# Half-unit, single-packet transfers for w_gate and w_up in a layer's forward and backward pass

## The chip, the cores and the metric

The kernel runs on one core of a Trainium2 chip. The metric is device time in microseconds (us) of the whole program, in runs without a disturbed clock; differences between kernels come from runs on the same chip in the same rounds. A profile is one execution under the hardware profiler. Its engines are PE (TensorE), DVE (VectorE), ACT (ScalarE), POOL (GpSimd) and SP (SyncE). Sixteen DMA engines move the data. Transfers reach them through three queues: q0, filled by GpSimd's software; q1, filled in hardware for SyncE; and q10, in hardware for ScalarE.

## The reference, cut to what matters

One token goes through a block with attention over the last 4096 positions of a cache and a gated feed-forward layer. Output and all gradients are wanted. Two gradients are of the whole cache, 4 heads x 65536 positions x 128, and are zero outside the last 4096 positions.

```python
# feed-forward part: D = 1024, F = 3584, all in bf16
g = einsum('bsd,df->bsf', x, w_gate)
u = einsum('bsd,df->bsf', x, w_up)
h = sigmoid(g) * u
y = einsum('bsf,fd->bsd', h, w_down)
...
_out, _vjp = jax.vjp(_f, A_x, A_k_cache, A_v_cache, A_wq, A_wo,
                     B_w_gate, B_w_up, B_w_down, c, w_mod)
return (_out, *_vjp(grad_out))
```

## The kernel before

Work is with single columns, so there is little arithmetic for each byte. Every weight is loaded once, used forward and backward, overwritten with its gradient in place, and stored. 120 stores of zeros (1024 KB each, rows of 8 KB) fill the cache gradients. They need no computed value and are spread over the program by hand-set lists: 61 go through GpSimd, some of them paced by a hand-set wait, and 59, in the feed-forward stage, through ScalarE without one.

The feed-forward stage has seven blocks of 512 columns. A *unit* is a block of one weight: 1024 KB. For w_gate and w_up it is 128 partitions x 8 rows of 1 KB. Five slots of 8 KB per partition are shared, so a load waits for the store of the gradient that was in its slot: w_gate of block n+1 for w_down's gradient of block n, w_up of n+2 for w_gate's, w_down of n+2 for w_up's.

```python
def load_wu(n):
    nc.gpsimd.dma_start(out=wu_t[n], in_=wu_view[:, :, n * FB:(n + 1) * FB])
def load_wg(n):
    nc.gpsimd.dma_start(out=wg_t[n], in_=wg_view[:, :, n * FB:(n + 1) * FB])
...
for n in range(NB):
    # ... PE: gate and up products; ACT: sigmoids; DVE: products; ACT: du_b, dg_b ...
    nc.sync.dma_start(out=wd_dram(out_8, n), in_=wd_t[n])     # w_down's gradient
    if n + 1 < NB:
        load_wg(n + 1)                                        # waits for that store
    for j in range(KD):
        ttr(wu[:, j, :], wu[:, j, :], du_b, dh2acc[...])      # DVE: row sums, backward
        last = outer_act(wu[:, j, :], h2[:, j:j + 1], du_b)   # ACT: the gradient, in place
        if j % 4 == 3:
            zero(Z_FFN[5 * n + 1 + j // 4], None, nc.scalar)  # zeros, issued by ACT
    nc.gpsimd.dma_start(out=dwu_view[:, :, n * FB:(n + 1) * FB], in_=wu)
    # ... the same for wg and dwg ...
    if n + 2 < NB:
        load_wu(n + 2)
        load_wd(n + 2)                                        # on SyncE
```

## Time and profile before

| | before |
|---|---|
| time, median of the first three runs | 653.28 us (651.76 to 654.0) |
| profiled span | 650.8 us |
| bytes moved | 262.63 MB |
| DMA engines busy, three queues together | 99.4% of the span |
| busiest compute engine (DVE) | 49% |

The page's first parts, its queues, its chain and the timeline of one block are shown in the prediction. Three more lines are from the list of transfers of the kernel before, with queue, count, size and the median time in us from issue to landing.

```profile
out_dram<-zeros ACTq DMA_DIRECT2D x59, 1024.0 KB, 20.9
arena<-in_B_w_up_dram POOLq DMA_DIRECT2D x7, 1024.0 KB, 14.5
arena<-in_B_w_gate_dram POOLq DMA_DIRECT2D x7, 1024.0 KB, 14.7
```

An estimate from the 425 GB/s that full slices of the GB/s row show: a unit of 1024 KB would take sixteen otherwise idle engines about 2.5 us. A w_gate load takes 14.7, as it shares them and queues behind others.

### The profile page before, as it was taken

The numbers are of one execution on the slowest core, as the hardware profiler recorded it, in microseconds if no ns is written. First come the engines' busy times: TensorE is split into PE (matmuls) and PEld (weight loads), VectorE is DVE, ScalarE is ACT, GpSimd is POOL, SyncE is SP. The second block draws the span as 40 slices with busy tenths as digits, with TensorE's granted clock in tenths as the row PEclk, the third lists the DMA queues.
The fourth block names the chain that finished last, engine by engine and source line by source line (L and its number), as shares of the span: only waits on it lengthen the run. The fifth ranks groups of instructions, "written<-read, shape, count | busy, mean of one in ns | idle before, by whom it ended". The sixth has DMA issues, their size and how long they took to land.

```text
span 650.8 us, 7106 instructions
## 1 busy us (share of the span) xinstructions
PE 149.7 (23%) x2784; PEld 127.4 (20%) x2784; DVE 319.7 (49%) x626; ACT 206.9 (32%) x306; POOL 83.0 (13%) x137
## 2 busy tenths in 40 slices
PE   3123227572201020010101101310670000424300
PEld 2123215572201020010101101300450000313200
DVE  3442005602737246081460814899700089996293
ACT  2000016611521613243133432789570000424800
POOL 2000000131010200102011010212111012112220
PEclk9999999865555555555555555575765555555555
DMA  8999999999999999999999999999999999999996
GB/s 335 430 428 422 426 426 413 404 418 397 421 425 415 416 417 393 414 388 408 417 356 419 361 409 415 392 382 412 388 415 422 415 425 426 425 407 388 410 411 251
DMA packets 43810, 262.63 MB, mean 404 GB/s; under 512 B 4096, under 2 KB 4096, under 8 KB 18432
## 3 DMA queue, kind: packets, MB, share of 16 engines
q0 software_dynamic: 23184, 131.08, 49.8%
q1 hardware_dynamic: 12048, 69.22, 26.0%
q10 hardware_dynamic: 8544, 61.88, 23.6%
q8 instruction: 22, 0.36, 0.2%
q14 instruction: 12, 0.10, 0.0%
HBM read 76.55 MB, written 185.60 MB: 403 GB/s over the span
## 4 chain that ended last, share of the span: by engine, by line
DMA 64%; DVE 14%; ACT 11%; PE 6%; issue 4%; POOL 0%; SPq 0%; POOLq 0%; ACTq 0%; DVEq 0%
DMA out_dram<-arena 28%; DMA arena<-in_B_w_gate_dram 18%; DMA arena<-in_w_mod_dram 7%; DVE arena L168 6%; DMA arena<-in_A_wq_dram 6%; ACT arena L172 5%; DMA arena<-in_A_k_cache_dram 5%; DVE junk L168 3%; PE tp_kv L342 2%; DVE arena L164 1%; ACT arena L345 1%; PE gu_ps L476 1%; ACT arena L230 1%; ACT du_b L508 1%; DMA out_dram<-dx_orow 1%
## 5 line engine op out<-in xcount | busy, mean ns | idle before, releaser
L168 DVE CUSTOM_DVE_ANT_0 arena<-arena 128x4096 bf16<-128x4096 bf16 (+1 forms) x24 | 80.1, 3350 | 51.4 <-DMA arena<-in_w_mod_dram 51.4
L476 PE MATMUL gu_ps<-h_bf,arena 128*128 128x1 bf16 x448 | 16.9, 172 | 192.1 <-DMA arena<-in_B_w_up_dram 103.5
L151 DVE TENSOR_TENSOR hh<-sg,gu_ps 128x4 f32<-128x4 f32 x7 | 1.1, 158 | 119.4 <-ACT om L481 119.4
L136 POOL DMA_DIRECT2D out_dram<-zeros x61 | 33.6, 554 | 185.0 <-PE q_ps L311 49.8
L476 PEld LDWEIGHTS <-arena 128*128 128x128 bf16 x448 | 16.2, 118 | 193.9 <-issue 166.7
L172 ACT ACTIVATE arena<-du_b,h 128x512 bf16<-128x512 bf16 x56 | 35.3, 710 | 36.0 <-DMA arena<-in_B_w_down_dram 32.3
L649 PEld LDWEIGHTS <-arena 8*128 8x128 bf16 x256 | 24.9, 127 | 106.1 <-issue 102.7
L172 ACT ACTIVATE arena<-dg_b,h 128x512 bf16<-128x512 bf16 x56 | 35.3, 708 | 26.4 <-issue 14.4
L345 ACT COPY arena<-tp_kv 128x1024 bf16<-128x1024 bf16 x13 | 13.1, 1010 | 89.7 <-PE tp_kv L342 89.7
L653 ACT CAST arena<-ps_kv 128x512 bf16<-128x512 f32 x32 | 16.1, 691 | 77.2 <-DMA out_dram<-arena 77.2
L168 DVE CUSTOM_DVE_ANT_0 junk<-arena,b1k 128x1024 bf16<-128x1024 bf16 x28 | 34.2, 1222 | 8.6 <-DMA arena<-in_B_w_down_dram 8.1
L168 DVE CUSTOM_DVE_ANT_0 arena<-arena,b1k 128x1024 bf16<-128x1024 bf16 x32 | 36.7, 1221 | 0.4 <-ACT b1k L230 0.4
L168 DVE CUSTOM_DVE_ANT_0 arena<-arena,du_b 128x512 bf16<-128x512 bf16 x56 | 34.8, 686 | 3.5 <-ACT du_b L508 3.5
L168 DVE CUSTOM_DVE_ANT_0 arena<-arena,dg_b 128x512 bf16<-128x512 bf16 x56 | 34.8, 685 | 0.0
L172 ACT ACTIVATE arena<-b1k,o_col 128x1024 bf16<-128x1024 bf16 x32 | 33.4, 1142 | 0.0
L649 PE MATMUL ps_kv<-DO_hd,arena 8*128 8x128 bf16 x128 | 15.3, 280 | 77.9 <-ACT arena L653 77.2
L342 PE MATMUL tp_kv<-ident_bf,arena 128*128 128x128 bf16 x256 | 22.1, 252 | 20.7 <-DMA arena<-in_A_k_cache_dram 13.0
L160 DVE COPY arena<-tp_kv 128x1024 bf16<-128x1024 bf16 x19 | 13.0, 690 | 28.1 <-PE tp_kv L342 28.1
L480 ACT ACTIVATE sg<-gu_ps 128x4 f32<-128x4 f32 x7 | 1.2, 174 | 76.3 <-PE gu_ps L476 76.3
L342 PEld LDWEIGHTS <-arena 128*128 128x128 bf16 x256 | 19.2, 115 | 23.6 <-DMA arena<-in_A_k_cache_dram 13.9
L429 POOL DMA_DIRECT2D arena<-in_B_w_up_dram x7 | 6.2, 890 | 134.4 <-DMA out_dram<-arena 134.4
L655 ACT ACTIVATE arena<-ps_kv 128x512 bf16<-128x512 f32 x32 | 16.1, 624 | 21.8 <-DMA out_dram<-arena 21.8
(185 smaller groups left out, 377.3 us busy)
## 6 DMA issues: line engine op xcount, KB each, us to landing
out_dram<-zeros POOLq DMA_DIRECT2D x61, 1024.0 KB, 20.4
out_dram<-zeros ACTq DMA_DIRECT2D x59, 1024.0 KB, 20.9
out_dram<-arena POOLq DMA_DIRECT2D x46, 1024.0 KB, 20.8
arena<-in_A_wq_dram SPq DMA_DIRECT2D x16, 1024.0 KB, 21.1
arena<-in_w_mod_dram SPq DMA_DIRECT2D x8, 1536.0 KB, 29.9
arena<-in_A_wo_dram SPq DMA_DIRECT2D x8, 1024.0 KB, 22.2
arena<-in_w_mod_dram SPq DMA_DIRECT2D x8, 1024.0 KB, 23.9
arena<-in_B_w_down_dram SPq DMA_DIRECT2D x7, 1024.0 KB, 11.9
```

The source lines that it names most:

```text
L136: ins = (q or nc.gpsimd).dma_start(out=zleft.pop(0), in_=zeros[:, :])
L160: return nc.vector.tensor_copy(out=out, in_=a)
L164: return nc.vector.tensor_scalar(out=out, in0=a, scalar1=s1, scalar2=None, op0=op0)
L168: return nc.vector.tensor_tensor_reduce(out=out, in0=w, in1=b, scale=1.0, scalar=0.0, op0=ALU.mult, op1=ALU.add, accum_out=acc)
L172: return nc.scalar.activation(out=out, in_=b, func=ACT.Copy, scale=col)
L230: last = nc.scalar.copy(out=o, in_=ps[:, :])
L342: nc.tensor.transpose(tp[:, t8 * P:(t8 + 1) * P], src[:, g, t_ * DH:(t_ + 1) * DH], ident_bf[:, :])
L345: last = nc.scalar.copy(out=o, in_=tp[:, :])
L476: nc.tensor.matmul(gu[:, half * 4 + jj:half * 4 + jj + 1], lhsT=w[:, j, jj::4], rhs=h2_bf[:, j:j + 1], start=(j == 0), stop=(j == KD - 1))
L649: nc.tensor.matmul(ps[:, t4 * DH:(t4 + 1) * DH], lhsT=rows[32 * g:32 * g + HG, t_ * P:(t_ + 1) * P], rhs=hd[32 * g:32 * g + HG, :], start= ...
L653: nc.scalar.copy(out=o, in_=ps[:, :])
L655: nc.scalar.activation(out=o, in_=ps[:, :], func=ACT.Copy, scale=float(scale))
```

## The change

The intent: with one packet for each engine's part of a half unit, the load should keep an engine for the whole of that packet instead of giving it up to zeros after each 4 KB; and a gradient's first half should leave while the second is being made. Half units keep a packet within 32 rows per engine.

```diff
     def load_wu(n):
-        nc.gpsimd.dma_start(out=wu_t[n], in_=wu_view[:, :, n * FB:(n + 1) * FB])
+        for k in range(0, KD, 4):
+            nc.gpsimd.dma_start(out=wu_t[n][:, k:k + 4, :], in_=wu_view[:, k:k + 4, n * FB:(n + 1) * FB],
+                                single_packet=True)
 ...  (load_wg likewise)
             if j % 4 == 3:
+                nc.gpsimd.dma_start(out=dwu_view[:, j - 3:j + 1, n * FB:(n + 1) * FB], in_=wu[:, j - 3:j + 1, :],
+                                    single_packet=True)
                 zero(Z_FFN[5 * n + 1 + j // 4], None, nc.scalar)
-        nc.gpsimd.dma_start(out=dwu_view[:, :, n * FB:(n + 1) * FB], in_=wu)
 ...  (dwg likewise)
```

More of the change, by code (lines that the diff above doesn't have):

```diff
@@ L428, in load_wu @@
     def load_wu(n):
-        nc.gpsimd.dma_start(out=wu_t[n], in_=wu_view[:, :, n * FB:(n + 1) * FB])
+        for k in range(0, KD, 4):
+            nc.gpsimd.dma_start(out=wu_t[n][:, k:k + 4, :], in_=wu_view[:, k:k + 4, n * FB:(n + 1) * FB],
+                                single_packet=True)
     def load_wg(n):
-        nc.gpsimd.dma_start(out=wg_t[n], in_=wg_view[:, :, n * FB:(n + 1) * FB])
+        for k in range(0, KD, 4):
+            nc.gpsimd.dma_start(out=wg_t[n][:, k:k + 4, :], in_=wg_view[:, k:k + 4, n * FB:(n + 1) * FB],
+                                single_packet=True)
     load_wd(0)
@@ L518 @@
             if j % 4 == 3:
+                nc.gpsimd.dma_start(out=dwu_view[:, j - 3:j + 1, n * FB:(n + 1) * FB], in_=wu[:, j - 3:j + 1, :],
+                                    single_packet=True)
                 zero(Z_FFN[5 * n + 1 + j // 4], None, nc.scalar)
-        nc.gpsimd.dma_start(out=dwu_view[:, :, n * FB:(n + 1) * FB], in_=wu)
         for j in range(KD):
@@ L524 @@
             if j % 4 == 3:
+                nc.gpsimd.dma_start(out=dwg_view[:, j - 3:j + 1, n * FB:(n + 1) * FB], in_=wg[:, j - 3:j + 1, :],
+                                    single_packet=True)
                 zero(Z_FFN[5 * n + 3 + j // 4], None, nc.scalar)
-        nc.gpsimd.dma_start(out=dwg_view[:, :, n * FB:(n + 1) * FB], in_=wg)
         if n + 2 < NB:
```

## The prediction

> **What bounds the kernel now.** I read the page's first two parts first, to see whether an engine or the transfers set the time; then the queues; then the chain of waits, which needs the first answer to be read properly; then the stage that the change touches, in the table by windows and the timeline.
>
> ```profile
> span 650.8 us, 7106 instructions
> PE 149.7 (23%) x2784; PEld 127.4 (20%) x2784; DVE 319.7 (49%) x626; ACT 206.9 (32%) x306; POOL 83.0 (13%) x137
> DMA  8999999999999999999999999999999999999996
> GB/s 335 430 428 422 426 426 413 404 418 397 421 425 415 416 417 393 414 388 408 417 356 419 361 409 415 392 382 412 388 415 422 415 425 426 425 407 388 410 411 251
> DMA packets 43810, 262.63 MB, mean 404 GB/s; under 512 B 4096, under 2 KB 4096, under 8 KB 18432
> q0 software_dynamic: 23184, 131.08, 49.8%
> q1 hardware_dynamic: 12048, 69.22, 26.0%
> q10 hardware_dynamic: 8544, 61.88, 23.6%
> ```
>
> No compute engine is over half busy, but the DMA row is at 9 nearly everywhere, and the three queues' packet times add to 99.4% of the sixteen engines' span. So the engines that move data are the bound, from the second slice to the last but one. At the good slices' 426 GB/s the 262.63 MB would take 616 us; the rest of the 651 us is slow moving rather than idleness. 120 of the transfers are stores of zeros, 1024 KB each, which depend on nothing but a place in a queue: they fill every gap.
>
> ```profile
> DMA out_dram<-arena 28%; DMA arena<-in_B_w_gate_dram 18%; DMA arena<-in_w_mod_dram 7%; DVE arena L168 6%; DMA arena<-in_A_wq_dram 6%; ACT arena L172 5%; DMA arena<-in_A_k_cache_dram 5%; DVE junk L168 3%; PE tp_kv L342 2%; DVE arena L164 1%; ACT arena L345 1%; PE gu_ps L476 1%; ACT arena L230 1%; ACT du_b L508 1%; DMA out_dram<-dx_orow 1%
> ```
>
> The chain names loads of w_gate (18%, 117 us), and reading it alone one would promise a large gain. But these loads are slow because zeros share the engines with them; the bytes remain.
>
> In the feed-forward stage, from the POOL and ACT timelines:
>
> ```profile
> 182.74 0.91 POOL L432 DMA_DIRECT2D arena<-in_B_w_gate_dram  x1 [21.52 <-DVE dhh L168]
> 183.64 0.90 POOL L520 DMA_DIRECT2D out_dram<-arena  x1
> 184.53 0.89 POOL L526 DMA_DIRECT2D out_dram<-arena  x1
> 213.32 0.89 POOL L429 DMA_DIRECT2D arena<-in_B_w_up_dram  x1 [27.90 <-DMA out_dram<-arena]
> 220.89 0.89 POOL L432 DMA_DIRECT2D arena<-in_B_w_gate_dram  x1 [6.68 <-DMA out_dram<-arena]
> 221.77 0.89 POOL L520 DMA_DIRECT2D out_dram<-arena  x1
> ...
> 184.27 8.91 ACTq L136 DMA_DIRECT2D out_dram<-zeros  x3
> 198.10 0.17 ACT L480 ACTIVATE sg<-gu_ps 128x4 f32<-128x4 f32 x1 [14.73 <-PE gu_ps L476]
> ```
>
> Two things are to be seen. POOL issues in program order: the w_up gradient is stored right after the next w_gate load (182.74 then 183.64; 220.89 then 221.77), and that load waits for the w_down gradient to land in the slot it needs. And ACT, which issues the zeros of this stage, is held for 8.91 us by three of them before it can do its next sigmoid.
>
> **What the Trainium skill says.** "DMA: Bandwidth & Descriptors", section "Queues, rings and completion order": each engine takes turns between queues by whole packets. The trace agrees: with w_gate or gradient packets of 4 KB on q0 against zeros of 8 KB on q10, in 187 to 205 us the packet records show 623 against 603, turn by turn, so q0 gets a third of the bytes. Section "SWDGE vs HWDGE vs iDMA" of the same page gives a packet as preferably up to 4096 B and at most 64 descriptors; in the trace the w_gate and w_up packets are 4096 B, four rows of 1 KB. Half a unit is 32 rows per engine, so it fits one packet of 32 KB. Section "Why small descriptors are slow" says that joining descriptors pays only up to 256 B; the trace has the numbers to check this, below. Its section "Rules for kernel authors" says that transfers issued from SP, ACT and GpSimd all run on the same 16 engines and interleave; the queue shares above agree.
>
> **The change part by part.**
> (a) Packet overhead. In the packet records the commonest durations are 84 ns for 2 KB, 159 for 4 KB, 309 for 8 KB and 460 for 12 KB: 150.5 ns per 4 KB and about 8.5 ns per packet. The 28 MB of w_gate, w_up and their gradients are 7168 packets of 4 KB; they become 896 of 32 KB. Saved: 6272 x 8.5 ns / 16 engines = 3.3 us. Against it, 28 more transfers each add one 9 ns completion packet per engine: 0.25 us. Net -3.1 us.
> (b) Share of an engine. A 32 KB packet takes about 8 x 150.5 + 8.5 = 1.21 us, against 0.31 us of a zero packet: q0 goes from a third to four fifths of the engine while it has work. A w_gate load now takes 14.7 us (median). It should take some 4.5 us from issue to its first packet (182.74 to 187 in the packet records), 2 x (1.21 + 0.31) = 3 us of moving, and some 2 us for the slowest engine: 9 to 10 us. Six loads on the chain save about 30 us of waiting there.
> (c) Where (b) goes. The zeros wait instead, and ACT holds them. Counting zeros issued against bytes moved on q10, the backlog never exceeds 6.6 MB before ACT stalls. Each unit block issues 4 to 11 zeros (59 in all), so in time its work is (6 + zeros) x 2.47 us at 425 GB/s: 35 to 42 us, against loop times of 38 to 41 us now. The chain can run ahead only until the backlog is full; then sigmoid and casts wait for zeros. I count zero net, except that the dip around 360 to 370 us, where the engines are about 89% busy, should fill: -1 us.
> (d) Reads that are no longer mixed. From 160 to 163 us almost only w_gate and w_up move, at 352 GB/s, 188 ns per 4 KB; mixed with zeros in 187 to 205 us they take 160 ns. With four fifths of the engine the loads are closer to alone. All 11 loads that come inside the loop at the slow rate would cost 11 x 16 x 28 ns = 4.9 us; I take half, +2.5 us.
> (e) Issue. A unit costs POOL 0.89 us, a zero 0.53; a half should be about 0.7, so +14 us of POOL in a stage of 245 us in which it is busy 20 us. Off the path: 0.
> (f) "Leaves as soon as made": POOL comes to the first stores only after the w_gate load, by which time most of both gradients is made. What ACT finishes late (2.92 us of waiting at 225.58) gains a little, behind a busy queue: 0.
> (g) The slot of w_down is free sooner, since its load waits for the w_up gradient to land; it moves out of the way of the w_down store. Chain shorter, bytes the same: 0, as in (c); perhaps -1 us for less waiting at the stage's end.
> Sum: -3.1 - 1 + 2.5 - 1 = -2.6 us: 650 to 651 us.
>
> **The rivals.** First, the chain decides: (b) and (g) come through and the loop falls to 30 us or less; the time would be 610 to 630. For it speaks the 18% of the chain; against it the 99.4% of packet time, since nothing in the change removes bytes. Second, better mixing cures the slow spells. The table by windows has 321 GB/s for 246 to 249 us at full occupancy, and packet times in this stage exceed their usual values by 10 us; if large packets removed most of that, 641 to 643. Against it: similar spells fall at 455 and 570 us, outside this stage, around the start of a load on q1 among stores. Third, the other way: long packets hold back q1, whose w_o rows go in 2 KB packets and whose w_down loads and stores are on the path, or ACT is held so long that first halves come late and the engines run empty: +5 to +12 us, 658 to 665.
>
> **Range and chances.** The bound is shown by three views, and no part of the change moves more than 5 us of it, so 650 us with 641 to 660 eight times in ten. Faster by over 2% means under 640.2 us, for which the second rival would have to come whole, or the first in part: 0.12. Slower means over 666.3: 0.06. Within 2%: 0.82.
>
> **What would show it.** Right: the DMA row stays at 9; the packets fall by some 5800 net to about 38,000; loads of halves land in about 10 us; w_gate's share of the chain drops to near 10% while zeros land later than their 20.9 us and ACT's stalls in issuing them grow; the mean rate stays within 400 to 409 GB/s. (d) is wrong if loads in the loop show no slower bytes than now. The whole is wrong if the mean rate rises beyond 412 GB/s, or if slices of the DMA row fall under 9 in this stage.

## The result, and the profile after

| | before | changed |
|---|---|---|
| median, four runs each | 653.5 us (651.76 to 654.0) | 654.75 us (653.72 to 655.64) |
| ratio, 95% interval | 1 | 1.0023 (0.9999 to 1.0047) |
| profiled span | 650.8 us | 652.0 us |

Ratios here are the mean time of one kernel's runs over that of the other's runs of the same rounds, so not quite the ratio of the medians. The change is the same as the kernel before within 2%, and a small loss is likelier than a gain. I had predicted 650, a gain of half a per cent. The time is inside the range; the gain did not come.

The page of the changed kernel, the lines that answer to those shown of before:

```profile
span 652.0 us, 7191 instructions
PE 151.6 (23%) x2784; PEld 128.4 (20%) x2784; DVE 319.5 (49%) x626; ACT 207.0 (32%) x306; POOL 100.8 (15%) x165
...
DMA  8999999999999999999999999999999999999996
...
DMA packets 44258, 262.63 MB, mean 403 GB/s; under 512 B 4544, under 2 KB 4544, under 8 KB 18880
...
q0 software_dynamic: 23632, 131.08, 49.8%
q1 hardware_dynamic: 12048, 69.22, 26.5%
q10 hardware_dynamic: 8544, 61.88, 23.1%
```

Read the packet line first, because it undoes most of the prediction. I expected some 5800 packets fewer, about 38,000. There are 448 more: 44,258 against 43,810. 448 is 28 more transfers times 16 engines, the 4-byte packets that report completion, and the count under 512 B shows just these (4096 to 4544). Nothing more was joined. In the packet records q0 has 10,240 packets of 4096 B, exactly as before, and none larger than 8192.

The shares of an engine did not change either. From 190 to 205 us in the changed kernel, when the w_gate load and the gradients of w_up and w_gate compete with zeros, the packet records show 516 packets of 4 KB on q0 and 514 of 8 KB on q10 (before, 536 and 505): still turn by turn, still a third of the bytes.

The list of transfers and the chain of the changed kernel:

```profile
out_dram<-zeros ACTq DMA_DIRECT2D x59, 1024.0 KB, 19.8
...
arena<-in_B_w_up_dram POOLq DMA_DIRECT2D x14, 512.0 KB, 13.1
arena<-in_B_w_gate_dram POOLq DMA_DIRECT2D x14, 512.0 KB, 12.4
```

```profile
DMA out_dram<-arena 32%; DMA arena<-in_B_w_gate_dram 14%; DVE arena L168 10%; DMA arena<-in_w_mod_dram 7%; DMA arena<-in_A_wq_dram 6%; DMA arena<-in_A_k_cache_dram 5%; DVE junk L168 2%; PE tp_kv L342 2%; DVE arena L164 2%; DMA out_dram<-zeros 2%; ACT arena L345 1%; ACT arena L172 1%; ACT arena L659 1%; PE gu_ps L480 1%; ACT du_b L512 1%
```

w_gate went from 18% to 14% of the chain and stores of gradients from 28% to 32%. Such a shift says little: the kernel below with the flag alone, whose packets are those of before, shows 14% for w_gate too. A half lands in 12.4 us, but each product sums over rows of both halves, so the second half is what the products wait for. Zeros land slightly sooner, not later as they would if loads had taken their turns.

POOL's timeline of the changed kernel shows the order of issue from the first block's gradients on:

```profile
181.96 1.53 POOL L435 DMA_DIRECT2D arena<-in_B_w_gate_dram  x2 [16.76 <-DVE dh2acc L168]
183.48 1.50 POOL L523 DMA_DIRECT2D out_dram<-arena  x2
184.97 1.50 POOL L530 DMA_DIRECT2D out_dram<-arena  x2
209.12 0.75 POOL L430 DMA_DIRECT2D arena<-in_B_w_up_dram  x1 [22.66 <-DMA out_dram<-arena]
215.40 0.76 POOL L430 DMA_DIRECT2D arena<-in_B_w_up_dram  x1 [5.52 <-DMA out_dram<-arena]
223.39 1.49 POOL L435 DMA_DIRECT2D arena<-in_B_w_gate_dram  x2 [7.24 <-DMA out_dram<-arena]
```

All four gradient halves leave together at 183 to 186 us, right after the w_gate load, as the whole units did at 183.64 and 184.53 before. In this block the early store exists in the program's text and not in time, and the next three blocks look the same; only in the last block, which has no w_gate load to wait for, do all four leave apart (406.67 to 417.88 us).

### The profile page after: what moved, and what is told of

The parts are those of the page before. It is cut to its first block, busy times and chain, and to the rows that moved or that the text cites. A ratio compares the mean times of both kernels' runs of the same rounds, so it can differ in the third digit from the quotient of the medians.

```text
span 652.0 us, 7191 instructions
## 1 busy us (share of the span) xinstructions
PE 151.6 (23%) x2784; PEld 128.4 (20%) x2784; DVE 319.5 (49%) x626; ACT 207.0 (32%) x306; POOL 100.8 (15%) x165
## 2 busy tenths in 40 slices
DMA packets 44258, 262.63 MB, mean 403 GB/s; under 512 B 4544, under 2 KB 4544, under 8 KB 18880
## 3 DMA queue, kind: packets, MB, share of 16 engines
q10 hardware_dynamic: 8544, 61.88, 23.1%
## 4 chain that ended last, share of the span: by engine, by line
DMA 65%; DVE 17%; ACT 6%; PE 5%; issue 3%; POOL 1%; ACTq 1%; SPq 0%; POOLq 0%; DVEq 0%
DMA out_dram<-arena 32%; DMA arena<-in_B_w_gate_dram 14%; DVE arena L168 10%; DMA arena<-in_w_mod_dram 7%; DMA arena<-in_A_wq_dram 6%; DMA arena<-in_A_k_cache_dram 5%; DVE junk L168 2%; PE tp_kv L342 2%; DVE arena L164 2%; DMA out_dram<-zeros 2%; ACT arena L345 1%; ACT arena L172 1%; ACT arena L659 1%; PE gu_ps L480 1%; ACT du_b L512 1%
## 5 line engine op out<-in xcount | busy, mean ns | idle before, releaser
L480 PE MATMUL gu_ps<-h_bf,arena 128*128 128x1 bf16 x448 | 18.3, 172 | 188.4 <-DMA arena<-in_B_w_up_dram 109.8
L172 ACT ACTIVATE arena<-du_b,h 128x512 bf16<-128x512 bf16 x56 | 35.2, 710 | 37.0 <-DMA arena<-in_B_w_down_dram 23.1
L659 ACT CAST arena<-ps_kv 128x512 bf16<-128x512 f32 x32 | 16.1, 692 | 79.4 <-DMA out_dram<-arena 79.4
L430 POOL DMA_DIRECT2D arena<-in_B_w_up_dram x14 | 10.6, 755 | 135.4 <-DMA out_dram<-arena 130.0
L160 DVE COPY arena<-tp_kv 128x1024 bf16<-128x1024 bf16 x19 | 12.9, 690 | 27.9 <-PE tp_kv L342 27.8
L342 PEld LDWEIGHTS <-arena 128*128 128x128 bf16 x256 | 18.4, 112 | 24.1 <-DMA arena<-in_A_k_cache_dram 13.9
L661 ACT ACTIVATE arena<-ps_kv 128x512 bf16<-128x512 f32 x32 | 16.1, 625 | 22.0 <-DMA out_dram<-arena 22.0
## 6 DMA issues: line engine op xcount, KB each, us to landing
out_dram<-arena POOLq DMA_DIRECT2D x36, 512.0 KB, 17.7
```

What stands on the lines that cost most here:

```text
L160: return nc.vector.tensor_copy(out=out, in_=a)
L172: return nc.scalar.activation(out=out, in_=b, func=ACT.Copy, scale=col)
L342: nc.tensor.transpose(tp[:, t8 * P:(t8 + 1) * P], src[:, g, t_ * DH:(t_ + 1) * DH], ident_bf[:, :])
L430: nc.gpsimd.dma_start(out=wu_t[n][:, k:k + 4, :], in_=wu_view[:, k:k + 4, n * FB:(n + 1) * FB], single_packet=True)
L480: nc.tensor.matmul(gu[:, half * 4 + jj:half * 4 + jj + 1], lhsT=w[:, j, jj::4], rhs=h2_bf[:, j:j + 1], start=(j == 0), stop=(j == KD - 1))
L659: nc.scalar.copy(out=o, in_=ps[:, :])
```

## The experiments

All are edits of the kernel before unless said otherwise. Theory A, formed from the packet line: the flag has no effect on the packets, so nothing of the change but the halving reached the chip; and the time is set by bytes and packets. Its rivals: the flag acts where packet sizes do not show it; or it is the chain, not the bytes, that sets the time.

### Does the flag do anything?

**The changed kernel without the flag.** Edit: `single_packet=True` removed everywhere.

> The changed kernel without the single-packet flag: half units and early stores alone. Theory A (the flag changes no packet on the GpSimd queue, as the 10,240 packets of 4096 B left in the changed kernel's trace say): 44,258 packets again, time within 0.3% of the changed kernel, so a ratio to the kernel before of 0.999 to 1.005. Rival B (the flag acts, but the trace does not show it in packet sizes): the ratio differs from 1.0023 by more than 0.005, or the landing of a half w_gate load moves by over 2 us.

Measured: 655.35 us, ratio 1.0038 (1.0022 to 1.0054). Packets 44,258, and a w_gate half lands in 12.1 us against 12.4. No effect of the flag is seen: both intervals overlap, and the landing moved by 0.3 us.

**The flag alone, on whole units.**

```diff
-        nc.gpsimd.dma_start(out=wu_t[n], in_=wu_view[:, :, n * FB:(n + 1) * FB])
+        nc.gpsimd.dma_start(out=wu_t[n], in_=wu_view[:, :, n * FB:(n + 1) * FB], single_packet=True)
 ...  (the same for wg, dwu, dwg)
```

> The kernel before with the flag alone, on whole units (64 rows of 1 KB per engine). Theory A: 43,810 packets as before, ratio 1.000 within 0.3%, w_gate landing 14.7 us within 1 us. Rival B: larger packets or a shorter landing, under 12 us, or a time off by over 0.5%.

Measured: ratio 1.0012 (0.9995 to 1.0030), and the packets are those of before:

```profile
DMA packets 43810, 262.63 MB, mean 402 GB/s; under 512 B 4096, under 2 KB 4096, under 8 KB 18432
```

w_gate landed in 16.1 us instead of 14.7, a little outside the 1 us that I allowed, and in the direction that no working flag would give; w_up landed in 13.9 against 14.5.

**The flag on another queue: w_o, which SyncE loads in rows of 2 KB.**

```diff
-        nc.sync.dma_start(out=wo_t[q4], in_=wo_view[:, q4 * 4:(q4 + 1) * 4, :])
+        nc.sync.dma_start(out=wo_t[q4], in_=wo_view[:, q4 * 4:(q4 + 1) * 4, :], single_packet=True)
```

> The kernel before with the flag on the eight w_o loads, which SyncE issues (2 KB rows, 4096 packets of 2048 B before). If the flag acts on the hardware-generated queue: the packets fall by about 3,970 to about 39,840 (8 loads x 16 packets of 64 KB), the w_o loads land sooner than 22.2 us and the zeros beside them later; time within 0.5%. If the flag acts nowhere: 43,810 packets and 22.2 us.

Measured: ratio 1.0004 (0.9984 to 1.0023), 43,810 packets, w_o lands in 21.9 us against 22.2. Nothing. So the flag changed no packet on GpSimd's queue or on SyncE's. Whether it reached the DMA engines and was not heeded, or was dropped on the way, no run shows.

**w_gate's halves through SyncE, with the flag.**

```diff
     def load_wg(n):
-        nc.gpsimd.dma_start(out=wg_t[n], in_=wg_view[:, :, n * FB:(n + 1) * FB])
+        for k in range(0, KD, 4):
+            nc.sync.dma_start(out=wg_t[n][:, k:k + 4, :], in_=wg_view[:, k:k + 4, n * FB:(n + 1) * FB],
+                              single_packet=True)
```

> The kernel before with w_gate loads issued by SyncE as two halves with the flag; everything else as before. If the flag acts on this queue: q1 gets 32 KB packets, a w_gate half lands in 5 to 8 us instead of 14.7, and w_gate's 18% of the chain falls under 10%. My theory that total bytes set the time then says: still 645 to 660 us. The rival that the chain sets it says 600 to 630 us. If the flag does not act: 1 KB packets against 8 KB of zeros, landing over 25 us and a time over 665 us.

Measured: 670.09 us, ratio 1.0296 (1.0255 to 1.0337). Its packets:

```profile
DMA packets 49298, 262.63 MB, mean 394 GB/s; under 512 B 4208, under 2 KB 11376, under 8 KB 23920
...
q1 hardware_dynamic: 19440, 76.56, 28.5%
```

q1 got 7168 packets of 1024 B, one for each row: this queue joined nothing, neither these rows with the flag nor the 2 KB rows of w_o with and without it. (GpSimd's queue joins four rows to 4 KB, flag or not.) From 250 to 255 us there are 249 of these against 219 zero packets of 8 KB, turn by turn, so the load gets about an eighth of the bytes. A half lands in 19.4 us rather than the 25 that I named, and the slower chain did cost time, as the third expectation said. The table by windows of this kernel (after the window: PE, weight loads, DVE, ACT, POOL, granted clock, DMA share, GB/s) shows how:

```profile
375.00:380.00 5.00, 2.02 (x40) 1.67 (x39) 4.83 (x12) 1.07 (x2) 1.15 (x1) 0.50 0.17 68
425.00:430.00 5.00, 0.00 (x0) 0.00 (x0) 5.00 (x17) 5.00 (x10) 0.89 (x1) 0.50 0.06 23
```

At 17% and 6% occupancy the DMA engines had run out of work: w_gate came so late that ACT had no place from which to issue the next zeros. That is read from ACT's timeline, which has none issued from 365.95 to 382.83 us and from 412.62 to 429.87; no run tested it apart. So the chain is not irrelevant. It costs when it lets the engines run empty.

### Do bytes set the time?

**Twelve zero stores fewer in the feed-forward stage.**

```diff
-    zleft = list(zregions)
+    zleft = list(zregions)[:len(zregions) - 12]
-Z_FFN = [0, 2, 0, 3, 5, 2, 0, 0, 2, 6, 1, 1, 0, 1, 5, 0, 0, 3, 1, 4, 2, 2, 2, 2, 0, 0, 3, 7, 1, 0, 0, 0, 0, 4, 0]
+Z_FFN = [0, 2, 0, 3, 3, 2, 0, 0, 2, 4, 1, 1, 0, 1, 3, 0, 0, 3, 1, 2, 2, 2, 1, 1, 0, 0, 3, 5, 1, 0, 0, 0, 0, 4, 0]
```

> The kernel before without 12 of the 59 zero stores in the feed-forward stage (two of its outputs are then not fully zeroed, on purpose: a wrong result in those places is possible). If the bytes moved set the time of this stage: 12 x 1.0486 MB at 425 GB/s is 29.6 us less, 622 to 626 us. If the chain of loads and stores sets it: only what the chain gains from lighter traffic, under half of it, 638 to 650 us, and the DMA row falls below 9 in that stage.

Measured: 627.64 us against 652.71, ratio 0.9606 (0.9583 to 0.9630): 25 us less, 85% of the 29.6. That is 1.6 us above the range that I gave for bytes, and 10 below the range for the chain. One output, with regions left unwritten, compares as not a number, on purpose; the others are right. Of the missing part, some may be engines that began to wait: the DMA row of this page falls from 9 to 8 in two slices of the stage, and the account below finds about 3.6 us more of empty time, as much as it differs by between profiles of kernels with the same data packets.

```profile
DMA  8999999999999999899999899999999999999996
```

### What does a larger share for the loads give?

The flag was to give the loads a larger share. As it did nothing, I gave it in another way: smaller packets for the zeros that the loads compete with, 4 KB instead of 8, which makes q0's share a half instead of a third.

**Zeros as two transfers of 512 KB each.**

```diff
+            reg = zleft.pop(0)
+            if q is not None:                       # ACT's zeros
+                for x in (0, ZW // 2):
+                    q.dma_start(out=reg[:, x:x + ZW // 2], in_=zeros[:, x:x + ZW // 2])
+                continue
 ...  (GpSimd's zeros as before)
```

> The kernel before with the 59 zero stores of ActE cut into two of 4 KB rows each: q0 with its 4 KB packets gets half of an engine instead of a third, which is the effect on shares that the single-packet flag was meant to have. If bytes and packet overhead set the time: w_gate lands in 9 to 12 us instead of 14.7, and the time rises by 7,552 x 8.5 ns / 16 = 4.0 us, to a ratio of 1.004 to 1.008. If the chain sets it: five w_gate loads that are 3 to 5 us shorter give a ratio of 0.965 to 0.98.

Measured: 667.17 us, ratio 1.0221 (1.0205 to 1.0236). w_gate did land sooner, in 11.5 us, and yet 14 us were lost, where I expected 4 from packet overhead. Who waited, 165 to 410 us (engine and line, releaser: us in total, times, longest), before and then in this kernel, and one such wait in ACT's timeline:

```profile
ACT sg L480 <- PE gu_ps L476: 76.3, 7, 14.7
```

```profile
ACT sg L485 <- DMA out_dram<-zeros: 86.6, 4, 27.0
...
ACT sg L485 <- PE gu_ps L481: 4.0, 1, 4.0
```

```profile
232.51 27.18 ACTq L139 DMA_DIRECT2D out_dram<-zeros  x10
259.74 0.17 ACT L485 ACTIVATE sg<-gu_ps 128x4 f32<-128x4 f32 x1 [26.99 <-DMA out_dram<-zeros]
```

Before, the sigmoid waited 76.3 us in this stage for the products, that is for loads. Here it waits 86.6 us for ACT's own zeros. ACT was held while many of its transfers were outstanding (27.18 us for the ten above). With 8 KB rows the backlog reached 6.6 transfers of 1 MB (zeros issued less bytes moved); here 7.4 transfers, but of half the size, 3.7 MB. So the cushion that keeps the engines fed had nearly halved, and they ran dry: 88% busy from 255 to 275 us. Running dry is the largest part and not the whole: of the 14.4 us between the two profiles the account below puts 4.8 down to packets, 3.4 to slower packets and 6.2 to empty engines.

**The same rows in one transfer of 1024 KB.** This takes the halved transfers out again.

```diff
-            ins = (q or nc.gpsimd).dma_start(out=zleft.pop(0), in_=zeros[:, :])
+            out, src = zleft.pop(0), zeros[:, :]
+            if q is not None:
+                out = out.rearrange("p (a x) -> p a x", a=2)
+                src = zeros[:, None, 0:ZW // 2].broadcast_to([P, 2, ZW // 2])
+            ins = (q or nc.gpsimd).dma_start(out=out, in_=src)
```

> The kernel before with ActE's 59 zero stores each still one transfer of 1024 KB, but made of 4 KB rows. With two transfers each of 512 KB the time was 667 us: the backlog of zeros that ActE could have outstanding fell from 6.6 MB to 3.7 MB, so that ActE was held up to 27 us ahead of a sigmoid, and the engines ran dry. Theory T (the limit counts transfers): backlog back at 6 to 7 MB, the engines stay at 9, time 655 to 659 us (4 us of packet overhead), w_gate lands in 9 to 12 us. Theory D (it counts row descriptors): backlog 3 to 4 MB again, and 663 to 670 us.

Measured: 655.94 us, ratio 1.0054 (1.0034 to 1.0075), 3.5 us over before, where 4.0 had been worked out from 8.5 ns a packet. The time is in the range of theory T, but the backlog reached 5.2 MB, between the two theories' figures, so what exactly is limited stays open: the most outstanding was 6.6 transfers before, 7.4 halved ones in the kernel with two, and 5.2 in this one. w_gate landed in 12.9 us, later than the 9 to 12 expected, though its share was as meant: from 186.3 to 191.3 us q0 and q10 have 255 and 256 packets of 4 KB. The chain of this kernel:

```profile
DMA out_dram<-zeros 16%; DMA out_dram<-arena 14%; ACTq L140 9%; ACT arena L176 9%; DMA arena<-in_w_mod_dram 7%; DVE arena L172 6%; DMA arena<-in_A_wq_dram 6%; DMA arena<-in_A_k_cache_dram 5%; DMA arena<-in_B_w_gate_dram 4%; DVE junk L172 3%; PE tp_kv L346 2%; ACT arena L349 1%; ACT arena L234 1%; DVE arena L168 1%; DMA out_dram<-dx_orow 1%
```

Is the 18% of w_gate worth anything? Here it fell to 4% of the chain, 117 us to about 26, and the program got slower by about the packets added. But most of that fall is not faster loads, which landed only 1.8 us sooner each: zeros took w_gate's place (16%, and 9% of ACT being held). In the waits of 165 to 410 us the sigmoid waited 76.3 us for products before; here it waited 37.5 us for zeros, 40.7 with no releaser in the profile, and 2.8 for products:

```profile
ACT sg L484 <- issue: 40.7, 2, 21.6
ACT sg L484 <- DMA out_dram<-zeros: 37.5, 2, 22.9
...
ACT sg L484 <- PE gu_ps L480: 2.8, 1, 2.8
```

The waiting changed its name and not its length.

### What do the halves cost?

| kernel | ratio to before | 95% interval |
|---|---|---|
| loads in halves | 1.0012 | 0.9987 to 1.0036 |
| stores in halves, when made | 1.0040 | 1.0021 to 1.0060 |
| stores in quarters, when made | 1.0030 | 1.0006 to 1.0053 |
| stores in halves, where the whole was | 1.0018 | 1.0001 to 1.0036 |

The edits are the parts of the change's diff, without the flag; for quarters, `j % 2 == 1` and slices of two rows; for the last, a loop over two slices at the old place of the store.

> The kernel before with only the loads of w_gate and w_up in two halves, no flag, stores whole. Halves without flag measured 1.0038 (1.0022 to 1.0054). Theory L (the cost is in the loads: two issues, 0.75 us apart on GpSimd, ahead of the w_gate wait, and two receipts): ratio 1.002 to 1.005. Theory S (the cost is in the stores): ratio within 0.001 of 1.

> The kernel before with only the gradient stores in two halves, each issued when made, no flag, loads whole. Theory S: ratio 1.002 to 1.005. Theory L: within 0.001 of 1. A rival gain (stores that leave early shorten the chain) would give under 0.999.

> The kernel before with the gradient stores in four pieces each, each issued when made, no flag. Halves cost 1.0040 (1.0021 to 1.0060). If the cost is one of each further transfer: three times as much, a ratio of 1.010 to 1.015. If it comes from leaving early, whatever the pieces: 1.002 to 1.006 again.

> The kernel before with the gradient stores in two halves, both issued where the whole store was issued. If the cost of store_halves is of the two transfers: 1.002 to 1.006. If it is of leaving early: within 0.0015 of 1.

The halved stores cost something like 0.2 to 0.4%, 1 to 3 us; the loads nothing clear. Quarters don't cost three times as much as halves, so it isn't a price of each transfer. Early and late differ by 0.2%, which the intervals do not separate, and 1.0012 for the loads and 1.0018 for the last run lie just outside both ranges that were expected of them. What makes this small cost stays open.

**The w_gate load behind the w_up stores.** The changed kernel with one call moved:

```diff
-        if n + 1 < NB:
-            load_wg(n + 1)
         for j in range(KD):
             ttr(wu[:, j, :], ...)              # the w_up half stores are in this loop
 ...
+        if n + 1 < NB:
+            load_wg(n + 1)
         for j in range(KD):
             ttr(wg[:, j, :], ...)
```

> The changed kernel with the next w_gate load moved behind the two w_up gradient stores on GpSimd, so that these really leave when made. My step (f) says that the position behind the w_gate load is why early leaving gains nothing, and that there is nothing to gain as the queue is busy: then 0.998 to 1.012 (the w_gate load now waits behind 1 MB on q0, up to 8 us an iteration, part of it hidden). If early leaving is worth something that the order hides: under 0.99.

Measured: 655.61 us, ratio 1.0051 (1.0022 to 1.0080). POOL's timeline of this kernel shows that w_up's halves now do leave as they are made:

```profile
174.70 0.76 POOL L521 DMA_DIRECT2D out_dram<-arena  x1 [9.94 <-ACT arena L172]
177.67 0.76 POOL L521 DMA_DIRECT2D out_dram<-arena  x1 [2.21 <-ACT arena L172]
181.87 1.50 POOL L435 DMA_DIRECT2D arena<-in_B_w_gate_dram  x2 [3.43 <-DMA out_dram<-arena]
```

The first is 9 us earlier than in the changed kernel, a half now lands in a median of 14.1 us instead of 17.7 (over 36 stores of that size), and nothing is gained. The loads paid for it: a w_gate half now takes 18.5 us to land instead of 12.4, so this run does not show early stores alone.

No experiment beat the kernel before. A version with zeros in 12 KB rows, which by the packet price should save some 2.7 us, did not fit in SBUF by 3.5 KB and was not run.

### One account for all of them

The packet records allow a sum. Give each packet the commonest duration of its size (46 ns for 1 KB, 84 for 2, 159 for 4, 309 for 8, 460 for 12; 9 ns for a completion) and divide by 16: that is the work. What packets took beyond that is slowness; what is left of the span is emptiness.

| profiled run | span | work | slowness | empty |
|---|---|---|---|---|
| before | 650.8 | 626.3 | 22.2 | 2.3 |
| changed | 652.0 | 626.6 | 23.0 | 2.4 |
| w_gate through SyncE | 667.0 | 629.2 | 20.8 | 17.0 |
| twelve zeros fewer | 625.6 | 596.5 | 23.1 | 6.0 |
| zeros as 2 x 512 KB | 665.2 | 631.1 | 25.6 | 8.5 |
| zeros in 4 KB rows | 655.7 | 630.5 | 23.3 | 1.9 |

The three columns make up the span by definition, so the table says where the time went and not why. One profile per kernel is a rough measure: the eight other kernels that have the data packets of before show 1.7 to 5.4 us of empty time. The change added 0.3 us of completion packets; its other difference, 0.8 us of slowness, is within what the slowness differs between kernels anyway (20.8 to 25.6 in this table). Row size moves the work column, bytes move it most, and a chain that is too slow moves the last. The table also bounds what a shorter chain could have given before: with the same packets at the same speed, no more than the 2.3 us of empty time.

## Why the prediction was right or wrong

Right: the bound. It named the transfers, not the chain, and 650 was to hold within 641 to 660. The DMA row stayed at 9, the mean rate went from 404 to 403 GB/s, and the time stayed. The signs that were to show the gain failed: 44,258 packets and not 38,000, halves landing in 12.4 us and not 10, zeros sooner and not later.

Wrong: the gain, and the first step that failed is **(a)**, "they become 896 of 32 KB". The premise was that the flag makes one packet of a half; I took it from the change's own words, and nothing in the profile of before could show it. The saving of 3.3 us was therefore 0, and 0.25 us for completions remained. With that and nothing from (c), (d) and (g) the prediction's own sum would have been +0.25 us instead of -2.6; +1.5 was measured, a difference within the interval of the ratio. The price per packet was right: 8.5 ns predicted 4.0 us for 7552 packets more, and 3.5 came.

**(b)** falls with it: the share stayed at a third and the six loads did not come 5 us sooner. **(d)**, slower unmixed reads at +2.5 us, falls for the same reason: w_gate and gradient packets still took 160 to 161 ns each from 190 to 205 us. It is not refuted, only never reached.

**(c)**'s principle, that the zeros wait instead and ACT holds them, fits the one kernel where a larger share was really given without starving the engines (zeros in 4 KB rows): the sigmoid's wait passed from the products to ACT's own zeros, with no gain. In the lines that the prediction shows of before, the hold of 8.91 us is not yet such a wait: it ends at 193.18 us, and the sigmoid at 198.10 was released by the products. The 35 to 42 us of (c) leave out the last block, whose 4 zeros give 25. Its -1 us for the dip at 360 to 370 us did not come: that window did fill, but a new dip took its place, as the windows show. Before, then changed:

```profile
335.00:340.00 5.00, 0.00 (x0) 0.00 (x0) 2.10 (x4) 3.71 (x6) 0.36 (x1) 0.50 0.98 324
360.00:370.00 10.00, 1.37 (x21) 1.02 (x18) 9.33 (x29) 4.87 (x7) 0.00 (x0) 0.50 0.89 325
```

```profile
335.00:340.00 5.00, 0.00 (x0) 0.00 (x0) 3.42 (x13) 0.00 (x0) 0.75 (x1) 0.50 0.78 320
360.00:370.00 10.00, 3.02 (x68) 2.61 (x68) 7.99 (x23) 4.63 (x8) 0.00 (x0) 0.50 1.02 365
```

The occupancy, the column before the last, rises from 0.89 to 1.02 in one window and falls from 0.98 to 0.78 in the other. Empty time is 2.3 and 2.4 us.

**(e)** a half was to cost POOL 0.7 us; it costs 0.75. POOL's busy time rose by 17.8 us instead of 14.

**(f)** was right that the stores stay behind the w_gate load (183.48 us). Freeing w_up's gained nothing, though that run delayed the w_gate loads too.

**(g)** w_down's load was to be issued sooner; SyncE's timeline has it at 204.23 us before and 204.93 in the changed kernel, and the four later ones come 1.5 to 3.2 us later as well. The -1 us did not come.

Of the rivals, the first (the chain decides) was not met by the change itself, whose loads kept their share. Against it stand the 2.3 us of empty time, which bound its gain unless packets get faster, and the kernel with fewer zeros, which kept 85% of what its bytes were worth. The second (fewer slow spells) did not happen: slowness went from 22.2 to 23.0 us. The third (ACT held by its zeros while engines run empty) did not happen in this change, but is what a larger share cost when the cushion was small.

## What to carry to other kernels

When the data engines are busy all the time and filler transfers take every free turn, a long wait on the chain can be only the place where a full queue shows; count bytes and packets first, and ask of a change whether it removes any, and of the chain only whether it ever lets the queues run empty. When a change rests on an option having an effect in hardware, find the number that must move if it acts (here the packet count) and look at that before any time. Order of issue on one engine can keep an "early" transfer from being early at all.

## What the Trainium skill lacked or had wrong

- "DMA: Bandwidth & Descriptors", section "SWDGE vs HWDGE vs iDMA", gives a packet as preferably up to 4096 B. In GpSimd's packet records that held where rows were joined (four rows of 1 KB, 10,240 packets of 4096 B), not for rows of 8 KB (10,880 packets of 8192 B). It doesn't say that SyncE's queue recorded each row alone here: 7168 packets of 1024 B for w_gate. Nor does any page name the option to ask for one packet, which changed nothing: 43,810 packets with and without it on whole units.
- The same page, section "Why small descriptors are slow", has joining pay only up to 256 B. Here four rows of 1 KB took 159 ns as one packet of GpSimd's queue and 4 x 46 = 184 ns as four of SyncE's, by the commonest durations. The price was about 8.5 ns a packet from 1 to 12 KB, and rows of 4 KB instead of 8 KB for 62 MB cost 3.5 us.
- No page gives a number for how many transfers an issuing engine may have outstanding before it is held. ScalarE was held at backlogs of 5.2 to 7.4 transfers, for up to 27 us.
